# A gated feed-forward layer: SyncE's queue in program order, sums of x behind the transposes' copies, four output tiles

## The chip, the core and the metric

The kernel runs on one core of a Trainium2 chip. A core has engines that each work off their own queue in order and wait for each other by semaphores: TensorE multiplies matrices (its weight loads run beside the multiplications), VectorE, ScalarE and GpSimd work element by element, and SyncE issues most of the transfers between the main memory and the core's own memory. TensorE writes its results into eight accumulator banks, each 128 partitions of 512 fp32 values; VectorE and ScalarE copy them from there or work on them. Times are microseconds of the device (us). The metric is the time of one execution, as the median of several; smaller is better. A change counts as faster or slower here when it moves the time by more than the measurement is uncertain.

## The reference

```python
# x: 1 x 2048 x 1024, w_gate and w_up: 1024 x 3584, w_down: 3584 x 1024, all bf16
def reference(x, w_gate, w_up, w_down):
    return (_gelu(x @ w_gate) * (x @ w_up)) @ w_down   # gelu in its tanh form
```

## The kernel before

The 2048 tokens are handled in two halves `h` of 1024, and each half in two token blocks of 512 (`TB`). A half has two stages.

**The gate and up stage** makes `hT`, the product of gelu(x @ w_gate) and x @ w_up, with the 3584 hidden features on the partitions: 28 tiles of 128 (`KF`). x must stand transposed for it (`xT`: eight tiles of 128 of the 1024 inputs, times 1024 tokens). The gate and up weights come in seven chunks of 512 features (`FG`), each chunk a 1 MB load for gate and one for up, in two buffers (`load_w`, L109). The first chunk of the first half is computed in plain form: `unit` (L174) runs eight matmuls for gate and eight for up, ScalarE makes the gelu (L163), VectorE the product (L167). All others are computed two feature tiles at a time by `pair_quads` (L292), a form with seven block products in place of eight (L298). This form needs sums of blocks: sums of x (`t_sums`, L244: t1, t2 and t3 on VectorE at L252, L253 and L255, a copy b22 on ScalarE at L254, t4 on GpSimd at L256), once for each half, and sums of weights (`s_sum`, L267, on GpSimd, with a copy on ScalarE at L287), for each pair, ahead of its use.

**The down stage** (`down`, L375) multiplies `hT` with w_down. It goes over two groups of 512 tokens. In each of them it takes 14 steps `kk`; a step uses one piece of w_down (`wd_sb`, two tiles of 128 features, 512 KB, three buffers, loaded by `load_wd`, L367) and runs 16 matmuls (L399) into all eight banks. At the last step each bank is copied into an output tile `o_sb` (bank 0, 2, 4, 6 on ScalarE at L411, the others on VectorE at L435), and each output tile is stored by SyncE (L438; in the last group of all the last tile goes in three parts, L415, L423 and L430). There are three output tiles in turn, and a group needs four.

**The start.** The first token block is not loaded transposed: it comes in two pieces as it stands (`load_x0_piece`, L114) and is transposed by TensorE (L205), and the results are copied to `xT` by VectorE (L185) and ScalarE (L187) in turn (`evac`, L183). `first_units` (L218) holds six banks open for three units of the first chunk, so that each group of matmuls can start as the weights and the transposed tiles of its `kd` arrive. The second token block is transposed on its way by the transfer itself (`load_xT`, L120). For the second half all of x comes that way, in 16 pieces.

**Between the halves.** The down stage of the first half has a list of fillers, one for each step: nothing, the loads of chunk 0 of the next half, the 16 transposing transfers (L488), the weight sums of the first pair, the loads of chunk 1, nothing, and `t_sums` of the next half. In step `kk` the program first loads down weights up to piece `kk + 2`, then runs the filler.

**What sets the order.** The program gives dependencies through tiles and buffers; a scheduler then puts the instructions of each engine, transfers included, into a queue of their own. It takes what it holds to be ready, by an order of priority that follows the program, so a later instruction can be placed ahead of an earlier one if it is held to be ready first. `tc.add_manual_dep` with `SCHED_DEP` adds an edge that counts for this placing alone and makes no wait on the chip. The kernel before uses it for TensorE's order at the start (L231). SyncE's queue and the place of the sums of x are left to the scheduler.

Of the kernel before, what the change touches and what calls it, by code (L numbers as in the profile page):

```python
# [13 lines left out]
SCHED_DEP = mybir.DependencyInfo(  # L14
    mybir.DependencyClass.NoSync, mybir.DependencyReason.SCHED_ONLY
)
# [15 lines left out]
def kernel(  # L32
# [8 lines left out]
    nc = tc.nc  # L41
    P = 128
    x2 = x.flatten_outer_dims()
# [6 lines left out]
    TB = 512  # L50
# [3 lines left out]
    FG = 512  # L54
# [4 lines left out]
    XQ = 512  # L59
# [7 lines left out]
    WDT = 2  # L67
# [3 lines left out]
    xv = x2.rearrange("t (ko ki) -> t ko ki", ki=P)  # L71
    wgv = w_gate.rearrange("(ko ki) f -> ki ko f", ki=P)
    wuv = w_up.rearrange("(ko ki) f -> ki ko f", ki=P)
    wdv = w_down.rearrange("(ko ki) d -> ki ko d", ki=P)
# [8 lines left out]
    wd_pool = ctx.enter_context(tc.tile_pool(name="wd", bufs=3))  # L83
    g_pool = ctx.enter_context(tc.tile_pool(name="g", bufs=4))
    m_pool = ctx.enter_context(tc.tile_pool(name="m5", bufs=1))
    o_pool = ctx.enter_context(tc.tile_pool(name="o", bufs=3))
    psum = ctx.enter_context(
        tc.tile_pool(name="psum", bufs=1, space=bass.MemoryType.PSUM)
    )
# [5 lines left out]
    def next_bank():  # L95
        b = banks[bank_ctr[0] % 8]
        bank_ctr[0] += 1
        return b


    xs0 = xs_pool.tile([P, TSB, D], BF16, name="xs")
    chunks = {}

    def new_chunk(key):
        wg_sb = wgu_pool.tile([P, KD, FG], BF16, name="wg_sb")
        wu_sb = wgu_pool.tile([P, KD, FG], BF16, name="wu_sb")
        chunks[key] = (wg_sb, wu_sb)

    def load_w(key, k0, k1, eng):  # L109
        c0 = key[1] * FG  # L110
        for w_sb, wv in zip(chunks[key], (wgv, wuv)):
            eng.dma_start(out=w_sb[:, k0:k1, :], in_=wv[:, k0:k1, c0 : c0 + FG])  # L112

    def load_x0_piece(q, eng):  # L114
        eng.dma_start(
            out=xs0[:, :, q * XQ : (q + 1) * XQ],
            in_=x2[0:TB, q * XQ : (q + 1) * XQ].rearrange("(ts p) d -> p ts d", p=P),
        )

    def load_xT(xT, h, tb, k0, k1):  # L120
        t0 = h * SH + tb * TB
        nc.sync.dma_start_transpose(  # L122
            out=xT[:, k0:k1, tb * TB : (tb + 1) * TB],
            in_=xv[t0 : t0 + TB, k0:k1, :],
        )

    xT = xT_pool.tile([P, KD, SH], BF16, name="xT")
    new_chunk((0, 0))
    load_x0_piece(0, nc.sync)
    load_w((0, 0), 0, WKP, nc.scalar)  # L130
    nc.scalar.preload_act_table(ACT.Gelu_apprx_tanh)
    ident = const_pool.tile([P, P], BF16, name="ident")
# [5 lines left out]
    for i in range(NWARM):  # L138
        b = banks[max(i - 1, 0)]
        warm.append(  # L140
            nc.tensor.matmul(b[:], lhsT=warm_l, rhs=warm_r, start=True, stop=True)
        )

    load_x0_piece(1, nc.sync)
    for k0 in range(WKP, KD, WKP):
        load_w((0, 0), k0, k0 + WKP, nc.sync)
    load_xT(xT, 0, 1, 0, KD)
    new_chunk((0, 1))
    load_w((0, 1), 0, KD, nc.sync)


# [27 lines left out]
        mult(hT, gelu(pss[0]), pss[1], key[1] * FPG + fi, tb)  # L179

    evac_ctr = [0]

    def evac(dst, src):  # L183
        if evac_ctr[0] % 2 == 0:
            nc.vector.tensor_copy(out=dst, in_=src)  # L185
        else:
            nc.scalar.copy(out=dst, in_=src)  # L187
        evac_ctr[0] += 1

    def transpose_x_piece(q):  # L190
# [48 lines left out]
    tsum = {}  # L239

    def half(j):
        return slice(j * KH, (j + 1) * KH)

    def t_sums(eng4):  # L244
        def b(j, l):
            return xT[:, half(j), l * TB : (l + 1) * TB]

        for name in ("t1", "t2", "t3", "t4", "b22"):
            tsum[name] = t_pool.tile([P, KH, TB], F32R, name=name)
        sub = ALU.subtract  # L250
        tt = nc.vector.tensor_tensor
        tt(out=tsum["t1"][:], in0=b(0, 1), in1=b(0, 0), op=sub)  # L252
        tt(out=tsum["t2"][:], in0=b(1, 1), in1=tsum["t1"][:].bitcast(F32), op=sub)  # L253
        nc.scalar.copy(out=tsum["b22"][:], in_=b(1, 1))  # L254
        tt(out=tsum["t3"][:], in0=b(1, 1), in1=b(0, 1), op=sub)  # L255
        eng4.tensor_tensor(  # L256
            out=tsum["t4"][:], in0=b(1, 0), in1=tsum["t2"][:].bitcast(F32), op=sub
        )
# [108 lines left out]
    def load_wd(n):  # L367
        if n >= NH * (SH // TB) * NKK:
            return
        k0 = (n % NKK) * WDT  # L370
        wd_sb = wd_pool.tile([P, WDT, D], BF16, name="wd_sb")
        nc.sync.dma_start(out=wd_sb[:], in_=wdv[:, k0 : k0 + WDT, :])
        wd_tiles.append(wd_sb)

    def down(hT, h, fillers):  # L375
        for grp in range(SH // TB):
            last_grp = h == NH - 1 and grp == SH // TB - 1
            o_sb = {}
            for kk in range(NKK):
                n = (h * (SH // TB) + grp) * NKK + kk  # L380
                while len(wd_tiles) < n + 3:
                    if n + 3 > NH * (SH // TB) * NKK:
                        break
                    if h == 0 and grp == 1 and len(wd_tiles) >= 2 * NKK:
                        break
                    load_wd(len(wd_tiles))
                if fillers:
                    fillers.pop(0)()
                wd_sb = wd_tiles[n]
                for b in range(8):  # L390
                    ts, dn = grp * TSB + b // 2, b % 2
                    c0 = dn * DN
                    r0 = h * SH + ts * P
                    split = last_grp and kk == NKK - 1 and b == 7
                    for cc, cw in (
                        [(c0, DN // 2), (c0 + DN // 2, DN // 2)] if split else [(c0, DN)]
                    ):
                        for c in range(WDT):
                            nc.tensor.matmul(  # L399
                                banks[b][:, cc - c0 : cc - c0 + cw],  # L400
                                lhsT=hT[:, kk * WDT + c, ts * P : (ts + 1) * P],
                                rhs=wd_sb[:, c, cc : cc + cw],
                                start=(kk == 0 and c == 0),
                                stop=(kk == NKK - 1 and c == WDT - 1),
                                skip_group_check=True,
                            )
                    if kk < NKK - 1:
                        continue
                    if dn == 0:
                        o_sb[b // 2] = o_pool.tile([P, D], BF16, name="o_sb")  # L410
                        nc.scalar.copy(  # L411
                            out=o_sb[b // 2][:, 0:DN], in_=banks[b][:]
                        )
                        if last_grp and b == 6:
                            nc.sync.dma_start(  # L415
                                out=out2[r0 : r0 + P, 0:DN], in_=o_sb[3][:, 0:DN]
                            )
                    elif split:
                        hh = DN // 2
                        nc.vector.tensor_copy(  # L420
                            out=o_sb[3][:, DN : DN + hh], in_=banks[b][:, 0:hh]
                        )
                        nc.sync.dma_start(  # L423
                            out=out2[r0 : r0 + P, DN : DN + hh],
                            in_=o_sb[3][:, DN : DN + hh],
                        )
                        nc.scalar.copy(  # L427
                            out=o_sb[3][:, DN + hh : D], in_=banks[b][:, hh:DN]
                        )
                        nc.scalar.dma_start(  # L430
                            out=out2[r0 : r0 + P, DN + hh : D],
                            in_=o_sb[3][:, DN + hh : D],
                        )
                    else:
                        nc.vector.tensor_copy(  # L435
                            out=o_sb[b // 2][:, DN:D], in_=banks[b][:]
                        )
                        nc.sync.dma_start(  # L438
                            out=out2[r0 : r0 + P, :], in_=o_sb[b // 2][:]
                        )  # L440


    for h in range(NH):
        hT = hT_pool.tile([P, KF, SH], BF16, name="hT")
        first_pair = 0
        if h == 0:
            first_units(hT)
            for fi in range(NSU, FPG):
                unit(hT, (0, 0), fi, 0)
            unit(hT, (0, 0), 0, 1)  # L450
            t_sums(nc.gpsimd)
            for fi in range(1, FPG):
                unit(hT, (0, 0), fi, 1)
            first_pair = PPG
            for name in S_NAMES:
                for j in range(2):
                    s_sum(0, first_pair, j, name)
# [11 lines left out]
        if h + 1 < NH:  # L469
            nh = h + 1  # L470
            xT = xT_pool.tile([P, KD, SH], BF16, name="xT")
# [15 lines left out]
            for tb in range(NTB):  # L487
                for kd in range(KD):  # L488
                    fillers.append(
                        lambda tb=tb, kd=kd: load_xT(xT, nh, tb, kd, kd + 1)  # L490
                    )
            fillers += [s_fill, w_fill1, lambda: None, lambda: t_sums(nc.gpsimd)]
        down(hT, h, fillers)


# [28 lines left out]
```

## Time and profile before

| what | value |
|---|---|
| time, median of 3 runs | 584.18 us (583.63 to 585.02) |
| profiled execution: its time | 583.31 us |
| profiled execution: span on the core | 581.5 us |
| matmuls of the pairs (L298) on the chain that ended last | 56% of the span |
| matmuls of the down stage (L399) on that chain | 31% |
| first half: gate and up stage, then down stage | to about 195 us, then to 304 us |
| second half: the same | to about 480 us, then to the end |
| mean granted clock of TensorE | 0.985 of full speed |

How to read the profile's lines below: the slices cut the span into 40 equal parts, and each digit is an engine's busy share in tenths (9 is 90% or more); PEclk is the clock that TensorE was granted, in tenths of full speed. PE is TensorE's multiplication, PEld its weight load, DVE VectorE, ACT ScalarE, POOL GpSimd, SPq the SyncE queue. A row of waits names who waited, for whom, the total in us, how often, and the longest. A row of the chain of waits has its start, its length, and what it was. A row of the timeline has start and length in us, engine, line, operation, output<-input, shapes and count, and in brackets the idle time of the engine before it and what ended that. A row of a table by stretches has the stretch, its length, the busy time (and count) of PE, PEld, DVE, ACT and POOL, the granted clock, the share of the DMA engines' time and GB/s. A row of transfers has the queue, the count, the size of one and the time from issue to landing.

### The profile page before, as it was taken

What the parts mean: (1) busy time and instruction counts of PE and PEld (TensorE: products, weight loads), DVE (VectorE), ACT (ScalarE), POOL (GpSimd) and SP (SyncE); (2) the same over time, 40 slices, a digit from 0 to 9 for tenths busy, and PEclk for the clock granted to TensorE, in tenths of its full rate; (3) what the DMA queues carried; (4) which work ended last, traced back from release to release, by engine and by line L of the source; (5) the groups of instructions that cost most, each with busy time, mean ns of one, the idle gap of its engine ahead of it and who ended that gap; (6) DMA issues with size and microseconds to landing.
All of it is one profiled execution on the core that took longest, in us unless ns stands there. A gap on an engine that the chain in (4) does not pass through costs nothing.

```text
span 581.5 us, 6767 instructions
## 1 busy us (share of the span) xinstructions
PE 559.9 (96%) x2523; PEld 336.3 (58%) x2523; DVE 176.2 (30%) x241; ACT 200.5 (34%) x343; POOL 248.8 (43%) x216
## 2 busy tenths in 40 slices
PE   7799999999999939999999999999999999999997
PEld 3246776776676514444447767776767774444443
DVE  0614334444434340010014344444344440001001
ACT  1414555455555210010015554555555550001001
POOL 0646677677677301000006776776777710000000
PEclk9799999999999969999999999999999999999999
DMA  9804404033040664464452404224040003446443
GB/s 277 265 1 144 145 2 145 26 120 122 23 146 0 161 194 159 172 210 154 145 180 74 144 1 146 71 74 145 0 145 3 0 1 108 145 148 236 159 146 108
DMA packets 60960, 67.54 MB, mean 116 GB/s; under 512 B 14592, under 2 KB 44672, under 8 KB 60928
## 3 DMA queue, kind: packets, MB, share of 16 engines
q1 hardware_dynamic: 60240, 66.53, 35.1%
q10 hardware_dynamic: 688, 0.59, 0.3%
q8 instruction: 20, 0.33, 0.2%
q14 instruction: 12, 0.10, 0.0%
HBM read 59.77 MB, written 4.19 MB: 110 GB/s over the span
## 4 chain that ended last, share of the span: by engine, by line
PE 91%; DMA 4%; SPq 3%; DVE 0%; ACT 0%; issue 0%; ACTq 0%; DVEq 0%
PE bank L298 56%; PE bank L399 31%; PE bank L153 4%; SPq L122 3%; DMA xT<-in_x_dram 1%; DMA out_dram<-o_sb 1%; DMA wu_sb<-in_w_up_dram 1%; DMA wd_sb<-in_w_down_dram 1%; DVE t L252 0%; ACT o_sb L411 0%; DVE xT L185 0%; ACTq L112 0%; ACT o_sb L427 0%; ACTq L411 0%; DVEq L252 0%
## 5 line engine op out<-in xcount | busy, mean ns | idle before, releaser
L399 PE MATMUL bank<-wd_sb,hT 128*128 128x512 bf16 x898 | 196.1, 381 | 9.7 <-DMA wd_sb<-in_w_down_dram 9.0
L298 PE MATMUL bank<-t,s 128*128 128x512 f32 x624 | 161.0, 406 | 0.0
L399 PEld LDWEIGHTS <-hT 128*128 128x128 bf16 x898 | 88.2, 98 | 117.3 <-issue 13.5
L298 PEld LDWEIGHTS bank<-t,s 128*128 128x128 f32 x624 | 117.4, 188 | 29.0
L277 POOL TENSOR_TENSOR s<-wg_sb 128x512 fp32r<-128x512 bf16 x26 | 31.8, 1224 | 175.6 <-PE bank L298 157.6
L167 DVE TENSOR_TENSOR hT<-g_sb,bank 128x512 bf16<-128x512 f32 x112 | 76.9, 688 | 75.0 <-ACT g_sb L163 31.1
L163 ACT ACTIVATE g_sb<-bank 128x512 f32<-128x512 f32 x112 | 66.6, 596 | 88.7 <-DVE bank L341 49.9
L411 ACT CAST o_sb<-bank 128x512 bf16<-128x512 f32 x16 | 9.4, 586 | 180.1 <-PE bank L399 172.9
L329 DVE TENSOR_TENSOR bank<-bank,m 128x512 f32<-128x512 f32 x52 | 36.4, 700 | 113.3 <-ACT bank L328 111.5
L435 DVE CAST o_sb<-bank 128x512 bf16<-128x512 f32 x15 | 10.4, 692 | 174.5 <-PE bank L399 170.3
L298 PE MATMUL bank<-xT,wg_sb 128*128 128x512 bf16 x208 | 53.9, 382 | 0.0
L298 PE MATMUL bank<-xT,wu_sb 128*128 128x512 bf16 x208 | 53.4, 379 | 0.0
L298 PE MATMUL bank<-b,s 128*128 128x512 f32 x208 | 51.4, 389 | 0.0
L298 PE MATMUL bank<-t,a 128*128 128x512 f32 x208 | 51.3, 389 | 0.0
L298 PEld LDWEIGHTS bank<-b,s 128*128 128x128 f32 x208 | 39.0, 188 | 8.2
L298 PEld LDWEIGHTS bank<-t,a 128*128 128x128 f32 x208 | 39.0, 188 | 8.1
L282 POOL TENSOR_TENSOR s<-wg_sb 128x512 fp32r<-128x512 bf16 x26 | 32.4, 1247 | 21.7 <-PE bank L298 21.7
L341 DVE TENSOR_TENSOR bank<-bank,m 128x512 f32<-128x512 f32 x52 | 36.4, 700 | 9.9 <-PE bank L298 9.9
L324 ACT COPY m<-bank 128x512 f32<-128x512 f32 x52 | 30.6, 588 | 17.6 <-PE bank L298 17.6
L328 ACT COPY bank<-bank 128x512 f32<-128x512 f32 x52 | 29.7, 571 | 17.0 <-PE bank L298 17.0
L298 PEld LDWEIGHTS <-wu_sb 128*128 128x128 bf16 x208 | 20.3, 98 | 24.7 <-issue 0.3
L320 ACT COPY bank<-bank 128x512 f32<-128x512 f32 x52 | 29.6, 571 | 13.4 <-PE bank L298 13.4
(33 smaller groups left out, 321.1 us busy)
## 6 DMA issues: line engine op xcount, KB each, us to landing
wd_sb<-in_w_down_dram SPq DMA_DIRECT2D x56, 512.0 KB, 3.2
wg_sb<-in_w_gate_dram SPq DMA_DIRECT2D x13, 1024.0 KB, 5.3
wu_sb<-in_w_up_dram SPq DMA_DIRECT2D x13, 1024.0 KB, 7.4
out_dram<-o_sb SPq DMA_DIRECT2D x15, 256.0 KB, 2.5
xs<-in_x_dram SPq DMA_DIRECT2D x2, 512.0 KB, 5.6
wg_sb<-in_w_gate_dram SPq DMA_DIRECT2D x3, 256.0 KB, 6.6
wu_sb<-in_w_up_dram SPq DMA_DIRECT2D x3, 256.0 KB, 6.8
xT<-in_x_dram SPq DMA_TRANSPOSE x17, 2.7
```

The lines of the kernel that those rows point to most:

```text
L153: return nc.tensor.matmul(ps[:], lhsT=w_sb[:, kd, fi * P : (fi + 1) * P], rhs=xT[:, kd, tb * TB : (tb + 1) * TB], start=(kd == 0), stop=(k ...
L163: nc.scalar.activation(out=g_sb[:], in_=ps[:], func=ACT.Gelu_apprx_tanh)
L167: nc.vector.tensor_tensor(out=hT[:, fc, tb * TB : (tb + 1) * TB], in0=g_sb[:], in1=ps[:], op=ALU.mult,)
L277: tt(out=t[:], in0=a(1, 0), in1=a(1, 1), op=ALU.add)
L282: tt(out=t[:], in0=a(0, 0), in1=a(1, 0), op=ALU.subtract)
L298: nc.tensor.matmul(banks[bank][:], lhsT=lhs[:, c, :], rhs=rhs[:, c, :], start=start and c == 0, stop=c == KH - 1, skip_group_check=True,)
L320: nc.scalar.copy(out=banks[QB[j]][:], in_=banks[PB[j]][:])
L324: nc.scalar.copy(out=m5[j][:], in_=banks[VB[j]][:])
L328: nc.scalar.copy(out=banks[RB[j]][:], in_=banks[QB[j]][:])
L329: nc.vector.tensor_tensor(out=banks[QB[j]][:], in0=banks[QB[j]][:], in1=m5[j][:], op=ALU.add)
L341: nc.vector.tensor_tensor(out=banks[VB[j]][:], in0=banks[RB[j]][:], in1=m5[j][:], op=ALU.add)
L399: nc.tensor.matmul(banks[b][:, cc - c0 : cc - c0 + cw], lhsT=hT[:, kk * WDT + c, ts * P : (ts + 1) * P], rhs=wd_sb[:, c, cc : cc + cw], st ...
```

## The change

Three things change. First, every transfer that SyncE issues goes through a new helper `sp`, which ties it behind the one before in the program, so the queue has the program's order. Second, a helper `after` ties t1 behind the last VectorE copy of a transposed tile, t3 behind t1, and the copy b22 behind the last ScalarE copy of a transposed tile; `evac` keeps these last copies in `last_evac`. Third, the pool of output tiles has four buffers in place of three. All edges are of the kind that counts for the placing alone. The transfers that ScalarE issues (L130, L430) stay as they are.

```diff
-    o_pool = ctx.enter_context(tc.tile_pool(name="o", bufs=3))
+    o_pool = ctx.enter_context(tc.tile_pool(name="o", bufs=4))
...
+    last_sp = [None]
+
+    def sp(inst):
+
+        if last_sp[0] is not None:
+            tc.add_manual_dep(
+                inst.ins, last_sp[0].ins.name, SCHED_DEP, reason="SP queue order"
+            )
+        last_sp[0] = inst
+        return inst
+
+    def after(inst, other):
+        tc.add_manual_dep(inst.ins, other.ins.name, SCHED_DEP, reason="engine order")
+        return inst
...
     def load_w(key, k0, k1, eng):
         c0 = key[1] * FG
         for w_sb, wv in zip(chunks[key], (wgv, wuv)):
-            eng.dma_start(out=w_sb[:, k0:k1, :], in_=wv[:, k0:k1, c0 : c0 + FG])
+            i = eng.dma_start(out=w_sb[:, k0:k1, :], in_=wv[:, k0:k1, c0 : c0 + FG])
+            if eng is nc.sync:
+                sp(i)
...
     def load_xT(xT, h, tb, k0, k1):
         t0 = h * SH + tb * TB
-        nc.sync.dma_start_transpose(
-            out=xT[:, k0:k1, tb * TB : (tb + 1) * TB],
-            in_=xv[t0 : t0 + TB, k0:k1, :],
+        sp(
+            nc.sync.dma_start_transpose(
+                out=xT[:, k0:k1, tb * TB : (tb + 1) * TB],
+                in_=xv[t0 : t0 + TB, k0:k1, :],
+            )
         )
...
+    last_evac = {}
 
     def evac(dst, src):
         if evac_ctr[0] % 2 == 0:
-            nc.vector.tensor_copy(out=dst, in_=src)
+            last_evac["dve"] = nc.vector.tensor_copy(out=dst, in_=src)
         else:
-            nc.scalar.copy(out=dst, in_=src)
+            last_evac["act"] = nc.scalar.copy(out=dst, in_=src)
         evac_ctr[0] += 1
...
-        tt(out=tsum["t1"][:], in0=b(0, 1), in1=b(0, 0), op=sub)
+        first = after(tt(out=tsum["t1"][:], in0=b(0, 1), in1=b(0, 0), op=sub), last_evac["dve"])
         tt(out=tsum["t2"][:], in0=b(1, 1), in1=tsum["t1"][:].bitcast(F32), op=sub)
-        nc.scalar.copy(out=tsum["b22"][:], in_=b(1, 1))
-        tt(out=tsum["t3"][:], in0=b(1, 1), in1=b(0, 1), op=sub)
+        after(nc.scalar.copy(out=tsum["b22"][:], in_=b(1, 1)), last_evac["act"])
+        after(tt(out=tsum["t3"][:], in0=b(1, 1), in1=b(0, 1), op=sub), first)
...
-        nc.sync.dma_start(out=wd_sb[:], in_=wdv[:, k0 : k0 + WDT, :])
+        sp(nc.sync.dma_start(out=wd_sb[:], in_=wdv[:, k0 : k0 + WDT, :]))
...
-                        nc.sync.dma_start(
+                        sp(nc.sync.dma_start(
                             out=out2[r0 : r0 + P, :], in_=o_sb[b // 2][:]
-                        )
+                        ))
```

The loads of the first token block (L115) and the stores of the last output tile (L415, L423) go through `sp` in the same way.

## What the change was predicted to do

> **What bounds the kernel now.** I read the page first: the share of each engine, then the slices.
>
> ```profile
> span 581.5 us, 6767 instructions
> PE 559.9 (96%) x2523; PEld 336.3 (58%) x2523; DVE 176.2 (30%) x241; ACT 200.5 (34%) x343; POOL 248.8 (43%) x216
> PE   7799999999999939999999999999999999999997
> PEclk9799999999999969999999999999999999999999
> ```
>
> TensorE is busy almost everywhere, so an edit gains only where TensorE stands still. A slice is 14.5 us. There are two such places: the first two slices, and the fifteenth (205 to 220 us), where the row of TensorE drops to 3. The granted clock drops in the second and the fifteenth slice. Next come the waits of TensorE, and the chain of waits through these places.
>
> ```profile
> PE bank L399 <- DMA wd_sb<-in_w_down_dram: 9.0, 1, 9.0
> PE bank L153 <- DVE xT L185: 5.7, 2, 5.6
> ...
> 7.61 8.11 DMA xT<-in_x_dram
> ...
> 15.85 2.29 DVE t L252
> 18.14 0.61 DVE xT L185
> ...
> 44.12 146.82 PE bank L298 x652
> ...
> 210.85 3.94 DMA wd_sb<-in_w_down_dram
> ```
>
> Two waits hold TensorE, 9.0 and 5.6 us (a third, of 0.7, comes below). At the start, VectorE sits on the sum t1 (L252) until the second token block of x has landed (7.61 + 8.11 = 15.72), runs it, and only then makes the copy of the TensorE transposes (L185) for which TensorE waits. The 9.0 us wait is for a piece of the down weights. The SyncE queue and TensorE's timeline show why, and what an idle stretch costs beyond itself.
>
> ```profile
> 10.88 1.06 PE L205 MATMUL bank<-ident,xs 128*128 128x128 bf16 x16
> 12.42 0.81 PE L153 MATMUL bank<-xT,wu_sb 128*128 128x512 bf16 x3
> 18.79 1.44 PE L153 MATMUL bank<-xT,wg_sb 128*128 128x512 bf16 x3 [5.56 <-DVE xT L185]
> 26.69 1.89 PE L153 MATMUL bank<-xT,wg_sb 128*128 128x512 bf16 x8
> 28.42 1.89 PE L153 MATMUL bank<-xT,wu_sb 128*128 128x512 bf16 x8
> 195.32 10.53 PE L399 MATMUL bank<-wd_sb,hT 128*128 128x512 bf16 x48
> 214.83 10.36 PE L399 MATMUL bank<-wd_sb,hT 128*128 128x512 bf16 x38 [8.98 <-DMA wd_sb<-in_w_down_dram]
> ...
> 18.79:24.75 5.96, 5.96 (x16) 2.15 (x15) 5.30 (x2) 1.24 (x2) 5.43 (x2) 0.53 1.08 372
> 214.83:219.00 4.17, 4.17 (x11) 1.48 (x11) 1.88 (x1) 0.00 (x0) 2.15 (x1) 0.51 1.08 375
> ...
> 190.04 20.70 SPq L122 DMA_TRANSPOSE xT<-in_x_dram  x16
> 210.85 0.52 SPq L372 DMA_DIRECT2D wd_sb<-in_w_down_dram  x1
> 211.47 0.40 SPq L112 DMA_DIRECT2D wu_sb<-in_w_up_dram  x1
> ```
>
> Down weights were loaded ahead for three steps of the down stage (48 matmuls of 16 a step). The fourth piece stands in SyncE's queue behind sixteen DMA transposes, 1.3 us each (20.70 / 16), and leaves at 210.85. Eight matmuls take 28.42 - 26.69 = 1.73 us, so 0.216 each. After the two idle stretches the granted clock is 0.53 and 0.51: fifteen matmuls take 5.96 us in place of 3.24 (2.72 lost), ten take 4.17 in place of 2.16 (2.0 lost). Each stretch thus costs its length and a cold restart.
>
> **The change part by part: the start.** t1 goes behind the last VectorE copy of a transpose, the b22 copy behind the last ScalarE one. Nothing is added but the order. The transposes of the second piece end at 10.88 + 1.06 = 11.94.
>
> ```profile
> 17.55 1.01 ACT L187 COPY xT<-bank 128x1024 bf16<-128x1024 bf16 x1
> ...
> 22.26 0.62 ACT L287 CAST a<-wu_sb 128x512 fp32r<-128x512 bf16 x1 [2.38 <-DMA wu_sb<-in_w_up_dram]
> 25.81 1.58 ACT L163 ACTIVATE g_sb<-bank 128x512 f32<-128x512 f32 x3 [2.93 <-PE bank L153]
> 5.53 0.47 SPq L112 DMA_DIRECT2D wu_sb<-in_w_up_dram  x1
> wu_sb<-in_w_up_dram SPq DMA_DIRECT2D x3, 256.0 KB, 6.8
> 34.92 1.16 POOL L285 TENSOR_TENSOR s<-wu_sb,s 128x512 fp32r<-128x512 bf16 x1
> ```
>
> The copies (0.61 on VectorE, 1.01 on ScalarE) then end at about 12.6 and 12.95, before TensorE has done what it has (12.42 + 0.81 = 13.23). So the 5.56 us go, and with them the 2.72 of the cold clock: **-8.28**. What is late next? The last weight piece, issued at 5.53, lands 6.8 us later at 12.3; its matmuls come two groups of 1.3 us after 13.1, at 15.7: covered. The second token block (15.72) is first used when the four held groups (5.2 us) and one unit of 16 matmuls (3.45) are through, at 21.7: covered by 6 us. GpSimd's last sum for the first pair ends at 36.1; the pair would start at 44.12 - 8.28 = 35.8, but uses that sum near its end: covered. Not covered is ScalarE's order. There the copy at 22.26 waits for a load and stands ahead of the first three gelus. TensorE reuses the first gelu's bank at 21.7. If that order stays, the first gelu ends at 22.26 + 0.62 + 0.53 (1.58 for three) = 23.4, a wait of 1.7 us; if the gelus go first (they are ready at about 17.7), nothing. The rows don't tell which, so I take the middle: **+0.9** (0 to 1.7). VectorE's t2 and t3, at t1's 2.3 us each, end at 22.7; the bank of its first product is wanted at 21.7 + 1.73 = 23.4, so that is a part of this term at most.
>
> **The SyncE queue.** In program order each step of the first down stage issues one piece of down weights, then one filler: nothing, the gate and up loads of the next half's chunk 0, and then sixteen transposes, one a step.
>
> ```profile
> wd_sb<-in_w_down_dram SPq DMA_DIRECT2D x56, 512.0 KB, 3.2
> 189.29 0.37 SPq L112 DMA_DIRECT2D wg_sb<-in_w_gate_dram  x1
> wg_sb<-in_w_gate_dram SPq DMA_DIRECT2D x13, 1024.0 KB, 5.3
> L372 SPq DMA_DIRECT2D wd_sb<-in_w_down_dram x1: 495/495/495, 212.0 to 212.0; - x1
> DMA to landing us min/median/max: 7.2/7.2/7.2
> ```
>
> A step lasts 10.53 / 3 = 3.5 us; its issues take 0.4 to 0.5 + 1.3 = 1.8 us, so SyncE keeps up. A piece is asked for two steps (7.0 us) before its use, as soon as its buffer is free, and needs 3.2 us: covered. The 8.98 us and the 2.0 of the cold restart go: **-11.0**. The three early pieces leave the start of the kernel for the gate and up stage, where there is room. But the chunk loads, which ran ahead of the transposes (one at 189.29), now stand between pieces. The piece issued at 212.0, behind a 1 MB load and another piece, took 7.2 us, so 2.1 MB took from 210.85 to 219.2, 8.35 us. In the new order it is 3.15 MB from a step's start. At about 0.37 MB a us (1.05 more: 2.8 us) the last piece lands after 11.2 us, and is wanted after three steps, at 10.4. That gives a wait of 0.8 to 1.3, once for chunk 0 and once for chunk 1 in the second group: **+2.0** (0 to 3). At the border of the two groups SyncE waits for the four output copies before the next piece: it leaves some 1.7 us after the border (my estimate from a copy of 0.6 us and the issue of stores at 0.5 each) and needs some 3.9, as the one at 210.85 did; it is wanted at 7.0: covered by 1.4. The sums of x for the second half can be taken up only when the transposes of steps ten to thirteen have landed, just where VectorE copies the outputs. If t1 (2.29 us) stands ahead of them, TensorE waits up to 2.3 us for a bank; I take 0, since the copies come first in the program, and keep 2.3 for the range.
>
> **Four output tiles.** Within a group the fourth tile no longer waits for the first store.
>
> ```profile
> 258.29 7.07 PE L399 MATMUL bank<-wd_sb,hT 128*128 128x512 bf16 x32 [0.74 <-ACT o_sb L411]
> 576.09 0.59 ACT L411 CAST o_sb<-bank 128x512 bf16<-128x512 f32 x1 [0.28 <-PE bank L399]
> 577.70 0.59 ACT L411 CAST o_sb<-bank 128x512 bf16<-128x512 f32 x1 [1.03 <-DMA out_dram<-o_sb]
> 578.18 0.38 ACT L427 CAST o_sb<-bank 128x256 bf16<-128x256 f32 x1
> ```
>
> At 258.29 TensorE waited 0.74 for it. In the last group ScalarE's copies come four matmuls (0.86) apart, so the one after 576.09 would start at 576.95 in place of 577.70, end at 577.54, and the last one would follow there in place of 578.18: 0.64 of the tail. **-0.74 and -0.64**, at no cost in time; the other stores hold nobody on TensorE.
>
> **The sum**: -8.28 - 11.0 - 0.74 - 0.64 = -20.7, and +0.9 + 2.0: -17.8. The profiled execution took 583.31 us (span 581.5 and 1.8 around it), so 565.5; the median of the runs shown is 0.87 above that execution, so **566.4**.
>
> **A cold clock after the new waits?** The rows show idle stretches of 5.56 and 8.98 us with a cold restart, and one of 0.74 us after which 32 matmuls took 7.07 us, 0.22 each, without one. Between 0.74 and 5.56 nothing is shown; in proportion (2.72 / 5.56 = 0.49 a us) my 2.9 us of new waits would cost 1.4 more, 567.8. I take none, since each new wait is nearer to the 0.74. [...]
>
> **Rivals.** (1) *The new waits are at their upper ends and cool the clock.* 1.7 + 3 + 2.3 = 7.0 in place of 2.9 gives 570.5; with 0.49 a us on top, 573.9. For it: SyncE, ScalarE and VectorE are strict queues, as both old stalls show. Chance 0.16. (2) *The start keeps a wait of the old length*, because the copies don't come first or another input of the held groups is late: 8.28 - 0.9 less gain, 573.8, and by the other terms a little more. Against it is the margin of the weight piece. Chance 0.05. (3) *Slower: the transposes wait for the load before them.* Once they did:
>
> ```profile
> SPq L122 <- DMA wu_sb<-in_w_up_dram: 1.6, 1, 1.6
> L122 SPq DMA_TRANSPOSE xT<-in_x_dram x8: 1151/1258/1262, 190.0 to 199.1; - x8
> ```
>
> If each transpose waited until the piece ahead of it had landed, a step on SyncE would be 3.2 + 1.3 + 0.4 = 4.9 us in place of 3.5: TensorE loses 1.4 in each of 16 steps, 22 us, and the time is 566.4 + 22 = 588. It decides from 17.8 / 16 = 1.1 us a step. Against it: the sixteen at 190 follow on each other by their own 1.26 us while the load issued at 189.29, of a kind that takes 5.3 us to land, was on its way. Chance 0.08. (4) *The order isn't what the edits say*, because the queue was in that order for another reason: 584.2, chance 0.04.
>
> **How the numbers follow.** Forecast, 562.8 to 570.5: 0.65. Below it: 0.02. With rival 1 the range is **562.8 to 573.9** (its low end is the sum without any new wait, 563.5, less 0.7, half the spread of the runs of before); it holds 0.81. Faster: 0.65 + 0.02 + 0.16 + 0.05 = 0.88. Rival 4 is within 0.2% (1.2 us, about what a measurement of this kernel can tell from no change) by 0.03. Slower: rival 3 and the rest of 4, 0.09.
>
> **What would show it.** Right: no wait of TensorE for L185 over 1 us; matmuls at 0.216 us from 13 us on; in SyncE's queue one transpose between two wd loads from about 195 on, no wd wait over 1.5 us; no ScalarE wait for out_dram. Wrong: a ScalarE copy of weights ahead of the gelus with a TensorE wait near 22 us; steps of the down stage over 3.5 us while transposes run; t1 ahead of the output copies near 235 us; or a granted clock under 1 anywhere after the start.

## The result, and the profile after

| kernel | median (range, runs) | ratio to before, 95% interval |
|---|---|---|
| before, beside the first runs of the change | 583.90 us (581.58 to 585.02, 4) | |
| changed | 568.08 us (566.82 to 569.15, 4) | 0.9733 [0.9694, 0.9772] |
| before, beside the repetition | 582.78 us (582.40 to 585.22, 9) | |
| changed, once more | 567.67 us (567.03 to 569.63, 5) | 0.9747 [0.9722, 0.9771] |

The forecast was 566.4 us in a range of 562.8 to 573.9. The profiled execution of the changed kernel took 569.15 us, its span is 567.4 us. Line numbers from here on are those of the kernel that a profile is of. First the page of the changed kernel: the span and the slices.

```profile
span 567.4 us, 6748 instructions
PE   8799999999999999999999999999999999999997
PEclk9899999999999999999999999999999999999999
```

The hole in the fifteenth slice is gone, and so is its cold clock. The second slice still has a 7, and its clock an 8. The waits of the changed kernel name what is left:

```profile
PE bank L176 <- ACT g_sb L186: 3.0, 1, 3.0
...
PE bank L423 <- DMA wd_sb<-in_w_down_dram: 1.2, 2, 0.7
```

The wait for the VectorE copy (5.6 us) has become one of 3.0 us for a gelu, and the 9.0 us for down weights have become 1.2 in two waits. The chain that ended last, of the changed kernel, gives the gain by stage:

```profile
24.44 0.60 ACT g_sb L186
...
40.74 151.35 PE bank L322 x672
...
199.05 7.58 DMA wd_sb<-in_w_down_dram
...
262.11 7.32 DMA wd_sb<-in_w_down_dram
...
290.35 176.40 PE bank L322 x784
```

The first pairs begin at 40.74 in place of 44.12: 3.4 us of gain at the start. The second half's pairs begin at 290.35 in place of 304.2, 13.9 us earlier, so 10.5 us come from what lies between, nearly all of it the first down stage. The remainder takes 277.05 us in place of 277.3. Together that is 14.1 us, the difference of the spans. The forecast had 7.4 for the start, 9.7 for the down stage and 0.6 for the end.

**The start.** ScalarE's and then TensorE's timeline of the changed kernel:

```profile
12.15 1.01 ACT L211 COPY xT<-bank 128x1024 bf16<-128x1024 bf16 x1 [4.45 <-PE bank L229]
15.89 1.90 ACT L278 CAST b<-xT 128x2048 fp32r<-128x2048 bf16 x1 [2.73 <-DMA xT<-in_x_dram]
21.17 0.62 ACT L311 CAST a<-wg_sb 128x512 fp32r<-128x512 bf16 x1 [3.39 <-DMA wg_sb<-in_w_gate_dram]
23.91 0.62 ACT L311 CAST a<-wu_sb 128x512 fp32r<-128x512 bf16 x1 [2.12 <-DMA wu_sb<-in_w_up_dram]
24.44 2.05 ACT L186 ACTIVATE g_sb<-bank 128x512 f32<-128x512 f32 x4
```

```profile
18.42 1.89 PE L176 MATMUL bank<-xT,wg_sb 128*128 128x512 bf16 x8
20.15 1.89 PE L176 MATMUL bank<-xT,wu_sb 128*128 128x512 bf16 x8
25.08 3.41 PE L176 MATMUL bank<-xT,wg_sb 128*128 128x512 bf16 x8 [3.04 <-ACT g_sb L186]
28.29 2.09 PE L176 MATMUL bank<-xT,wu_sb 128*128 128x512 bf16 x8
30.22 1.89 PE L176 MATMUL bank<-xT,wg_sb 128*128 128x512 bf16 x8
```

The copy of the transposes (12.15) now comes ahead of b22, and TensorE runs on without a gap to 22.04. The queue of ScalarE holds what the prediction named as not covered: the two copies of weights for the pairs (L311) stand ahead of the gelus, and the second waits for the up load until 23.91. TensorE waits 3.04 us, and the next eight matmuls take 28.29 - 25.08 = 3.21 us in place of 1.73, the eight after them 1.93: 1.7 us of cold clock on top. The wait is counted from the end of a matmul, which the profile estimates. The granted clock falls to 0.50 only at 25.3 us, 0.2 us after TensorE has started again.

**The first down stage.** SyncE's queue of the changed kernel, from the end of the first step on:

```profile
196.08 0.40 SPq L127 DMA_DIRECT2D wg_sb<-in_w_gate_dram  x1
196.58 0.52 SPq L127 DMA_DIRECT2D wu_sb<-in_w_up_dram  x1
199.05 0.37 SPq L396 DMA_DIRECT2D wd_sb<-in_w_down_dram  x1
199.51 2.00 SPq L144 DMA_TRANSPOSE xT<-in_x_dram  x1
202.50 0.37 SPq L396 DMA_DIRECT2D wd_sb<-in_w_down_dram  x1
202.92 1.14 SPq L144 DMA_TRANSPOSE xT<-in_x_dram  x1
...
210.73 2.98 SPq L144 DMA_TRANSPOSE xT<-in_x_dram  x1
```

One transpose stands between two pieces of down weights. The piece of 202.50 leaves 3.45 us after the one of 199.05, which is a step of 16 matmuls, and SyncE is through with both issues after 1.6 us: it keeps up. Two of the sixteen transposes, both after the 2 MB of chunk 0, hold the queue longer: 2.00 us at 199.51 and 2.98 at 210.73. The second nearly fills its step. The piece of 199.05 is the one behind the 2 MB of chunk 0. It landed after 7.58 us (the chain above), and TensorE waited 0.74 us for it; the one of 262.11, behind chunk 1, took 7.32 us and cost 0.49.

### The profile page after: what moved, and what is told of

It is laid out like the page before. It is cut to its first block, busy times and chain, and to the rows that moved or that the text cites. A ratio compares the mean times of both kernels' runs of the same rounds, so it can differ in the third digit from the quotient of the medians.

```text
span 567.4 us, 6748 instructions
## 1 busy us (share of the span) xinstructions
PE 557.3 (98%) x2523; PEld 335.6 (59%) x2523; DVE 175.2 (31%) x241; ACT 200.8 (35%) x343; POOL 248.3 (44%) x216
## 4 chain that ended last, share of the span: by engine, by line
PE 92%; DMA 5%; SPq 1%; ACT 0%; issue 0%; ACTq 0%; DVE 0%; DVEq 0%
PE bank L322 58%; PE bank L423 32%; DMA wu_sb<-in_w_up_dram 3%; PE bank L176 3%; DMA wd_sb<-in_w_down_dram 3%; SPq L144 1%; ACT g_sb L186 0%; SPq L127 0%; ACTq L127 0%; DVE o_sb L444 0%; ACT o_sb L451 0%; DVEq L444 0%; ACT a L311 0%; ACTq L186 0%
## 5 line engine op out<-in xcount | busy, mean ns | idle before, releaser
L423 PE MATMUL bank<-wd_sb,hT 128*128 128x512 bf16 x898 | 194.1, 379 | 1.2 <-DMA wd_sb<-in_w_down_dram 1.2
L423 PEld LDWEIGHTS <-hT 128*128 128x128 bf16 x898 | 87.7, 98 | 107.3 <-issue 2.3
L301 POOL TENSOR_TENSOR s<-wg_sb 128x512 fp32r<-128x512 bf16 x26 | 31.6, 1217 | 136.6 <-PE bank L322 93.9
L306 POOL TENSOR_TENSOR s<-wg_sb 128x512 fp32r<-128x512 bf16 x26 | 30.3, 1167 | 20.9 <-PE bank L322 20.9
L344 ACT COPY bank<-bank 128x512 f32<-128x512 f32 x52 | 29.6, 570 | 14.3 <-PE bank L322 14.3
```

The lines of the kernel that those rows point to most:

```text
L301: tt(out=t[:], in0=a(1, 0), in1=a(1, 1), op=ALU.add)
L306: tt(out=t[:], in0=a(0, 0), in1=a(1, 0), op=ALU.subtract)
L344: nc.scalar.copy(out=banks[QB[j]][:], in_=banks[PB[j]][:])
L423: nc.tensor.matmul(banks[b][:, cc - c0 : cc - c0 + cw], lhsT=hT[:, kk * WDT + c, ts * P : (ts + 1) * P], rhs=wd_sb[:, c, cc : cc + cw], st ...
```

## The experiments

**The same kernel again.** The first four runs lay in two pairs, 567.22 and 566.82 at a mean granted clock of 1.000, 568.93 and 569.15 at 0.997.

> The changed kernel once more, nothing edited. My theory: TensorE's wait of 3.04 us for the first gelu's bank near 22 us is at the edge of what cools its clock, so its runs fall into two groups, about 567 us at a mean granted clock of 1.000 and about 569 us at 0.997, some 1.7 us apart (what the cold restart cost in the profile). Rival: the spread has another source (the loads' landing); then time and granted clock don't go together, and the runs fill the span between 566.5 and 569.5 us.

The times were 567.03, 567.06 and 567.67 us at 1.000, and 569.42 and 569.63 at 0.997. This time the profile is of the first kind. TensorE's timeline in it:

```profile
5.52 1.89 PE L229 MATMUL bank<-ident,xs 128*128 128x128 bf16 x16 [0.74 <-DMA xs<-in_x_dram]
7.20 1.49 PE L176 MATMUL bank<-xT,wg_sb 128*128 128x512 bf16 x3
...
24.58 1.89 PE L176 MATMUL bank<-xT,wg_sb 128*128 128x512 bf16 x8 [1.63 <-ACT g_sb L186]
26.30 1.89 PE L176 MATMUL bank<-xT,wu_sb 128*128 128x512 bf16 x8
```

The wait is 1.63 us, and no matmul behind it is slow. But the first transposes and matmuls are (1.89 and 1.49 us; 1.07 and 0.81 in the other profile). They run at about half rate, as their lengths say; the granted clock of the profile stands at 1.00 there in both, so it doesn't show this. The wait is 1.4 us shorter for two reasons: TensorE comes to the gelu's bank 0.9 us later (22.95 in place of 22.04), and the up weights' copy starts 0.5 us earlier (23.42 in place of 23.91). The theory holds for the two groups, with a part it did not have: a slow start at 5.5 us makes the later wait shorter. The profiles of the other runs below that wait for a gelu agree: 1.54 us after a slow start (1.89 and 1.49 us), 1.79 after a late one (its second transposes begin at 12.04 us in place of 11.05), 3.13 after a fast one, and 1.94 after a fast one with another wait of 0.75 us ahead of it. The runs without a profile show time and mean clock alone, and what sets the start is not shown.

**The gelus ahead of the weight copies.** `last_gelu` keeps the latest gelu on ScalarE; the copies of the weights for the first pair are tied behind the fourth of token block 0.

```diff
-            nc.scalar.copy(out=t[:], in_=a(1, 1))
+            i = nc.scalar.copy(out=t[:], in_=a(1, 1))
+            if behind is not None:
+                after(i, behind)
...
                 unit(hT, (0, 0), fi, 0)
+            plain_gelu = last_gelu[0]
...
-                    s_sum(0, first_pair, j, name)
+                    s_sum(0, first_pair, j, name, plain_gelu)
```

> The two copies of weights for the first pair stand behind the four gelus of token block 0 in ScalarE's queue, all else as in the changed kernel. My theory (ScalarE's order is what TensorE waits for): the wait of 3.04 us near 22 us goes, and with it the cold restart of about 1.7 us in the runs that have one, so the span is 562.7 us against 567.4 us in the profile, the median near 565 us, and the granted clock 1.000 in every run. Rival 1 (VectorE is late next: t1 to t3 end at 22.7 us, the first product after them): up to 1 us of the wait stays, on the bank of the up matmuls. Rival 2 (the late landing of the loads itself holds TensorE): no gain, 568 us.

> The gelus first once more, to stand beside the three others on the same chip: 564 to 565 us, no run with TensorE waiting for a gelu's bank.

Measured were 564.46 us (564.06 to 565.64, ratio 0.9682 [0.9662, 0.9702]) and, later, 564.29 us (0.9680 [0.9662, 0.9698]). ScalarE's timeline of the first of them:

```profile
18.60 1.57 ACT L188 ACTIVATE g_sb<-bank 128x512 f32<-128x512 f32 x3 [0.71 <-PE bank L176]
21.41 0.60 ACT L188 ACTIVATE g_sb<-bank 128x512 f32<-128x512 f32 x1 [1.23 <-PE bank L176]
21.90 0.61 ACT L315 CAST a<-wg_sb 128x512 fp32r<-128x512 bf16 x1
23.74 0.62 ACT L315 CAST a<-wu_sb 128x512 fp32r<-128x512 bf16 x1 [1.23 <-DMA wu_sb<-in_w_up_dram]
```

The up load lands no earlier (23.74), but nobody on TensorE stands behind it any more: in neither profile does TensorE wait between 13 us and the down stage. So ScalarE's order was the cause; both rivals fall. The clock of 1.000 in every run did not come: it was 0.998 to 1.000, with no time that goes with it. Both profiles have 0.998, and from the first pairs on every piece of matmuls in their chains is within 0.03 us as long as in the repeated changed kernel at 1.000 (151.33, 6.94, 55.43, 20.88, 176.38 and 96.73 us).

**Each half of the change alone.** First the queue without the order of the sums (the three `after` calls of `t_sums` taken out), then the order of the sums without the queue:

```diff
-        if last_sp[0] is not None:
+        if False:
```

> SyncE's queue in program order and four output tiles, but the sums of x left to the scheduler. My theory: the old wait of 5.56 us for the VectorE copy and its cold restart of 2.72 us return, and the gelu's wait (3.04 us and 1.7 us cold) goes because the gelus come later anyway: 3.6 us more than the changed kernel's profiled execution, about 572 us. Rival (most of the start's gain was never there, since the gelu's wait stands in its place): within 1 us of the changed kernel, 568 us.

> The sums of x behind the copies and four output tiles, but SyncE's queue left to the scheduler; so three pieces of down weights are loaded at the start again, behind the second chunk. My theory: the wait of 8.98 us behind the sixteen transposes and its cold restart of 2.0 us return, the two waits of 0.74 and 0.49 us behind the chunk loads go: 9.8 us more than the changed kernel, 577 to 579 us. On the start: if the second chunk's up load landed late in the changed kernel (23.9 against 22.2 us) because nothing stood behind it in the queue, it lands at 22.2 to 22.4 us here and the gelu's wait is about 1.4 us; if its landing simply varies, or hangs on what TensorE does, it is 23.9 us and 3.0 us again.

The queue alone: 571.74 us (0.9805 [0.9786, 0.9825]). The sums alone: 577.27 us (0.9900 [0.9881, 0.9919]). TensorE's timeline of the first, then of the second:

```profile
18.93 0.94 PE L176 MATMUL bank<-xT,wg_sb 128*128 128x512 bf16 x3 [4.46 <-DVE xT L209]
19.67 1.49 PE L176 MATMUL bank<-xT,wu_sb 128*128 128x512 bf16 x3
20.95 1.49 PE L176 MATMUL bank<-xT,wg_sb 128*128 128x512 bf16 x3
```

```profile
24.81 1.89 PE L176 MATMUL bank<-xT,wg_sb 128*128 128x512 bf16 x8 [1.79 <-ACT g_sb L186]
...
210.30 84.98 PE L423 MATMUL bank<-wd_sb,hT 128*128 128x512 bf16 x385 [9.79 <-DMA wd_sb<-in_w_down_dram]
```

Each half removes its own stall, as both theories of the prediction have it, and the old stall returns where its half is missing, with cold matmuls behind it (in the first 1.49 us for three in place of 0.81; in the second 84.98 us for 385, which take 83.2 at 0.216 each). In the first it is 4.46 us in place of 5.56, with a later start: its second transposes begin at 12.12 us, those of the kernel before at 10.88. The guess on the late up load fell, though: with three pieces of down weights behind it, it was waited for until 23.65 us all the same.

**What delays the up load?** In the kernel before, its copy started at 22.26. The transfers of the profiles, by stretches of 3 us, hold a small thing: one packet of instructions (0.02 MB). Here it is in the repeated changed kernel, from 19 to 22 us:

```profile
q1 hardware_dynamic: 871, 0.88, 88.8%
q8 instruction: 1, 0.02, 2.3%
```

2.3% of sixteen engines for 3 us is 1.1 us of one engine. In the same profile the stretch from 22 to 25 us, in 40 slices of 0.075 us:

```profile
GB/s 14 27 27 27 14 27 27 27 27 14 27 14 0 0 0 0 0 0 0 0 0 0 0 0 0 0 0 0 0 0 0 0 0 0 0 0 0 0 0 0
DMA packets 21, 0.02 MB, mean 7 GB/s; under 512 B 1, under 2 KB 21, under 8 KB 21
```

The load is all there but for 21 packets of 1 KB that move one or two in a slice, at up to 27 GB/s, for 0.9 us. A sixteenth of the 372 GB/s in the prediction's row from 18.79 us on is 23, so this looks like what is left to one late engine. All twelve profiles, by the place of the packet (to a quarter of a us), with the times from issue to landing of the two loads of the second chunk (issued near 13.7 and 14.3 us):

| profile | packet from | gate load | up load | copy of the up weights starts |
|---|---|---|---|---|
| before | 24.0 | 5.7 | 8.0 | 22.26 |
| before with four tiles (below) | 24.25 | 5.8 | 8.2 | 22.48 |
| queue alone | 21.75 | 6.1 | 8.4 | 22.75 |
| sums alone | 19.5 | 5.7 | 9.2 | 23.65 |
| gelus first | 19.25 | 5.9 | 9.2 | 23.74 |
| split loads (below) | 19.25 | 5.8 | 9.2 | 23.54 |
| changed, again | 19.0 | 5.8 | 9.1 | 23.42 |
| both (below) | 18.75 | 5.8 | 9.0 | 23.28 |
| three tiles (below) | 18.75 | 5.7 | 9.0 | 23.42 |
| three tiles, t1 behind (below) | 17.25 | 7.5 | 9.6 | 24.01 |
| changed | 17.0 | 7.4 | 9.5 | 23.91 |
| gelus first, again | 16.5 | 6.9 | 9.0 | 23.30 |

Where the packet comes after the up load, that load lands soonest, in 8.0 and 8.2 us. Where it comes a us ahead of its end, the load takes 8.4 us; where it comes earlier, 9.0 to 9.6. The gate load is late, 6.9 to 7.5 us in place of 5.7 to 6.1, in the three with the earliest packets. The packet comes at 24 us where TensorE stood for 5.6 us at the old stall, at 21.75 where it stood for 4.46, and before 20 where that stall is gone: so the change itself seems to have moved it into the loads. No run set the packet's place by itself, so all this is argued and not shown. Over the whole run of the changed kernel its queue moves 20 packets with 0.33 MB, about 16.5 KB each.

**Three output tiles, in program order.**

> The changed kernel with three output tiles again. My theory: the wait of 0.74 us at the border of the first half's groups returns, and at the end the fourth ScalarE copy waits for a store again; 1.0 to 1.4 us more than the changed kernel's 565.3 us span (its profile without the cold restart), in program order perhaps more, since the stores now stand ahead of the next down weights in SyncE's queue. Rival: the tiles are worth nothing on TensorE (the border's wait was covered, only the end counts): 0.3 us more.

571.40 us (570.22 to 573.48, 0.9814 [0.9788, 0.9839]), and a profiled span of 568.4 us against 565.3: more than expected, 3.1 us. The timeline at the border of the first half's groups in this kernel:

```profile
241.71 2.29 DVE L276 TENSOR_TENSOR t<-xT 128x2048 fp32r<-128x2048 bf16 x1 [2.58 <-DMA xT<-in_x_dram]
241.96 0.59 ACT L435 CAST o_sb<-bank 128x512 bf16<-128x512 f32 x1 [3.37 <-DMA out_dram<-o_sb]
242.59 0.81 PE L423 MATMUL bank<-wd_sb,hT 128*128 128x512 bf16 x3 [0.75 <-ACT o_sb L435]
243.91 0.68 DVE L459 CAST o_sb<-bank 128x512 bf16<-128x512 f32 x1
244.65 3.83 PE L423 MATMUL bank<-wd_sb,hT 128*128 128x512 bf16 x17 [1.25 <-DVE o_sb L459]
```

The fourth tile waits for the first store (3.37 us), so the scheduler puts t1 of the second half ahead of VectorE's last copy, and TensorE waits another 1.25 us for that. That the one leads to the other is inferred from the order. With four tiles t1 stands behind it, as the changed kernel's VectorE timeline shows:

```profile
241.39 0.69 DVE L459 CAST o_sb<-bank 128x512 bf16<-128x512 f32 x1 [0.17 <-PE bank L423]
243.78 2.29 DVE L276 TENSOR_TENSOR t<-xT 128x2048 fp32r<-128x2048 bf16 x1 [1.69 <-DMA xT<-in_x_dram]
```

To see whether t1 is what costs, it was tied behind that copy (`last_o` keeps it), still with three tiles:

```diff
+        if last_o[0] is not None:
+            after(first, last_o[0])
```

> Program order with three output tiles, and t1 of the second half tied behind the first group's last VectorE copy of an output. My theory: most of the 3.7 us that three tiles cost in the run above come from t1, which stands ahead of that copy there (TensorE waits 1.25 us for it and 0.19 us for down weights that leave late); with t1 behind it the copy runs about 242.0, the wait for it is 0 to 0.2 us, the one of 0.75 us for ScalarE's copy stays, and the median is 1.2 to 1.6 us under 571.4 us. Rival: the store that SyncE waits for is what costs, whatever VectorE does; then the time stays near 571 us.

570.27 us (568.75 to 571.00, 0.9793 [0.9776, 0.9810]). At the border, in its timeline (t1 follows the copy of 244.38):

```profile
244.38 0.69 DVE L462 CAST o_sb<-bank 128x512 bf16<-128x512 f32 x1 [3.11 <-DMA out_dram<-o_sb]
...
245.00 7.28 PE L426 MATMUL bank<-wd_sb,hT 128*128 128x512 bf16 x32 [1.00 <-ACT o_sb L438]
```

The border costs 1.00 us in place of 0.75 + 1.25 + 0.19. The theory holds for the rows; the 1.00 that stays is the store's, as both last copies waited over 3 us for it. The median came down 1.1 us where 1.2 to 1.6 was expected, and the intervals of the two versions overlap, so the times alone don't tell them apart; this profile also has a gelu's wait of 3.13 us with a cold restart, which the one of three tiles has not. Last, four tiles in the kernel before, and nothing else:

> The kernel before with four output tiles and nothing else (only the last two stores change places). My theory: the wait of 0.74 us at 258 us and 0.3 to 0.6 us of the end go, 1.0 to 1.4 us less than before. Rival (the four tiles are worth as much here as under program order): 3 us less or more.

582.27 us against 582.57: ratio 0.9992 [0.9979, 1.0005], no difference that can be told. In its profile TensorE runs through the border without a wait, but the wait for down weights is 9.4 us in place of 9.0. The expected 1.0 us or more was not measured.

**The loads of the two chunks split over two steps.** The gate load goes in one filler, the up load in the next (`load_w1` issues one of the two; `w_fill` and `w_fill1` now issue the gate load alone):

```diff
-            fillers = [lambda: None, w_fill]
+            fillers = [w_fill, lambda: load_w1((nh, 0), 1)]
...
-            fillers += [s_fill, w_fill1, lambda: None, lambda: t_sums(nc.gpsimd)]
+            fillers += [s_fill, w_fill1, lambda: load_w1((nh, 1), 1), lambda: t_sums(nc.gpsimd)]
```

> The changed kernel, but the gate and the up load of each of the two chunks in the first down stage stand in two steps instead of one (gate in one step, up in the next; chunk 0 begins one step earlier). My theory: the two waits of TensorE for down weights (0.74 to 0.86 and 0.49 us) go, 1.2 to 1.4 us less. Rival: they come from the transposes beside them, not from 2 MB at once; then at least the first one stays.

> The gelus first and the split loads together. My theory: the gains add, 1.4 to 1.6 us less than the gelus alone (564.5 us), about 563.0 us; span near 561 us. Rival: what the loads give up is lost again at another wait; 564.5 us.

Alone: 565.48 us (565.41 to 565.52, 0.9700 [0.9682, 0.9718]). That is 2.2 to 2.6 us under the changed kernel's two medians, where 1.2 to 1.4 was expected. But no run of it has the group at 0.997; against the changed kernel's profile of the other group the span is 1.6 us shorter (563.7 and 565.3), and in neither profile did the wait for the gelu cool the clock. With the gelus first: 563.74 us (562.95 to 563.94, 0.9668 [0.9649, 0.9686]). The chain of the version with both:

```profile
37.00 151.33 PE bank L332 x672
188.33 96.71 PE bank L433 x448
285.04 176.38 PE bank L332 x784
461.42 96.73 PE bank L433 x450
```

From 13 us to the end TensorE waits for nothing; the first down stage takes 96.71 us, as long as the second. The split is what removes the two waits, with the transposes still beside the pieces, so that rival falls. Over the gelus alone (564.29) the gain is 0.55 us, short of the 1.4 to 1.6 expected, and within the intervals. By profiles with the same slow start the first down stage is 1.9 us shorter than with the gelus alone (96.71 in place of 98.61), and the span 1.8 (562.0 and 563.8). Both edits together beat the changed kernel; their intervals against before don't meet.

## Why the prediction was right, point by point

- *Both stalls go, with their cold restarts (-8.28 and -11.0).* Shown: with the queue alone a wait of 4.46 us stays at the start, with the sums alone one of 9.79 in the down stage.
- *The order on ScalarE (+0.9, 0 to 1.7).* The mechanism was named, its size was wrong. The order stayed as before, the upper case, and the up load came 1.2 to 1.7 us later than its row in the profile before. In the first profile 8.28 - 3.4 = 4.9 us of the start's gain are missing: 3.04 of wait and 1.7 cold. In the second 8.28 - (44.12 - 38.55) = 2.7 are missing. There the wait is 1.63, within the bound, and 0.9 is the slow start at 5.5 us, a term that the prediction did not have. The step that failed is the bound of 1.7, since it took the landing from the old row. In the first profile the start so misses its forecast by 4.0 us, more than the 3.7 by which the span's gain (14.1) falls short of the sum (17.8); the loads, below, gave 0.8 back. The median, 1.7 us above the forecast, lies between the two groups.
- *No new wait cools the clock.* Wrong in some runs. Waits of 3.04 and 3.13 us had a cold restart, waits of 1.94, 1.79, 1.63 and 1.54 us had none. That a wait nearer to 0.74 than to 5.56 us costs nothing more was the author's estimate, with no row between the two: a gap that the profile gives as 3.04 was enough. With the weights' copy ahead of the gelus and the clock under 1 after the start, two of the prediction's own signs of being wrong came in, although the time lay near the forecast.
- *Two waits behind the chunk loads (+2.0).* 0.74 and 0.49 us, 1.2 together; the split loads, which remove both, show the cause.
- *t1 ahead of the output copies (0, up to 2.3).* 0 was right, but for a reason the prediction didn't give: the fourth tile. With three tiles it cost 1.25 us.
- *Four tiles (-0.74 and -0.64).* The border's wait went. At the end about 0.3 of the 0.64 came: ScalarE's last copy now waits 0.32 us for VectorE's copy out of the same bank. In the new order three tiles cost some 3 us, so the four are worth more there than forecast, and nothing measurable in the kernel before.
- *Rival 3, transposes that hold the queue.* Shown wrong by SyncE's queue: 1.6 us of issues in a step of 3.45. Two of the sixteen transposes did take 2.0 and 3.0 us, and TensorE waited behind neither.

## What to carry to other kernels

When a stall is removed, the next instruction in each strict queue that waits for a transfer is the candidate for the new wait: look there for work that TensorE needs and that stands behind it. Price such a wait with a landing time that can move (here one load took 8.0 to 9.6 us), and with a cold restart where the waits measured had one (here 3.04 and 3.13 us had, 1.94 had not). In this kernel a queue in program order needed its big loads spread over the steps, and enough buffers that no store was waited for inside it.

## What the runs showed of the hardware

- An idle stretch of TensorE of 3.04 us, by the profile, was enough for a cold restart of 1.7 us; 1.94 us was not. The clock fell only after the stretch had ended, by 0.2 us there and by some 0.6 after the 4.46 us of the queue alone (0.90 on average from 17.5 to 20 us, 0.50 from 20 to 22.5); in the kernel before it fell within the 5.56 us, at 17.5.
- In two profiles of the same kernel the first sixteen transposes took 1.07 and 1.89 us, with a granted clock of 1.00 in both, and TensorE came 0.9 us later to the gelu's bank in the second; the wait there was 3.04 and 1.63 us.
- A packet of instructions, about 16.5 KB, took 2.0 to 2.4% of sixteen DMA engines for 3 us, 1.0 to 1.2 us of one. An up load during which it came landed after 8.4 to 9.6 us in place of 8.0 to 8.2 (that the packet is the cause is argued from twelve profiles).
- Between the halves of the changed kernel a transpose by transfer held SyncE's queue for 1.13 to 1.18 us in fourteen steps, and for 2.0 and 3.0 in two that came after 2 MB of loads.
